# Accumulating products on four column tiles in place of two, with the second pair's sum added by an identity product

## The chip, the cores and the metric

One core of a Trainium2 chip. The metric is the device time of one execution in microseconds (us); lower is better.

The profile calls TensorE PE (PEld is its loading of weights), VectorE DVE and ScalarE ACT. The granted clock is the share of TensorE's full speed that the throttle allows at a moment; in these traces it is 1.00 or 0.50. PSUM is the memory in which products accumulate, in banks. A round is a set of products that run side by side on different column tiles. The path is the chain of work and waits that sets the end.

## The reference, cut to what matters

```python
x = A_x                                     # 8 x 1 x 576, bf16
g = sigmoid((x * gate_w).sum(-1))
a = attention(x @ wq, last 2048 keys and values of each of 16 heads) @ wo    # wo: 4096 x 576
b = gelu(layernorm(B_x) @ w1 + b1) @ w2 + b2                                 # w2: 4608 x 576
return g * a + (1 - g) * b                  # 8 x 576
```

About 134 of the 154 MB that are read are keys and values (16 transfers of 4096 KB and 32 of 2048 KB). The output has only 8 rows: the final sum over `wo` and `w2` is a long series of products with 8 columns of weights (the rows of the batch) against 576 columns of data.

## The kernel before

All products of the two final projections accumulate in one PSUM bank. The 576 output columns are cut into NJ = 2 halves of JN = 288; half j goes to column tile 32j. So two products run at once, on the first two of four column tiles.

```python
class AccGroup:
    def __init__(self, name, mms, deps, cost, after=(), prio=0):
        ...
        def fn(e):
            for i, (lhsT, rhs) in enumerate(grp.mms):
                for j in range(NJ):
                    ins = e.matmul(ps[32 * j:32 * j + 8, BK_ACC, 0:JN], lhsT, rhs[:, JN * j:JN * j + JN],
                                   start=False, stop=True, skip_group_check=True, tile_position=(0, 32 * j))
            return ins
...
def project():                      # output projection: 8 groups of 8 products
    for c in range(4):
        for ch in (c, c + 4):
            dst, d = wo_here[ch // 2]
            mms = [(oT[:, ch, j, :], dst[:, ch % 2, D * j:D * j + D]) for j in range(4)]
            AccGroup("proj%d" % ch, mms, place_done[c] + [d], cost=1.0)
...
def m2_chunk(ci):                   # w2 in 4 chunks; the last in 3 pieces of 4, 4 and 1 rows
    cuts = [0, 4, 8, 9] if ci == FC - 1 else [0, FJ]
    for n, (j0, j1) in enumerate(zip(cuts, cuts[1:])):
        d = dma("sp", w2_fn, ...)
        mms = [(hT[:, FJ * ci + j, :], dst[:, j * D:(j + 1) * D]) for j in range(j0, j1)]
        ops.append(AccGroup("m2_%d_%d" % (ci, n), mms, [o_hT, d], cost=0.16 * (j1 - j0), after=o_m2[-1:]).op)
...
# end: VectorE casts half 0 and ScalarE half 1 out of PSUM, each sends its half
```

A small list scheduler orders the operations of each engine from their estimated costs (`cost`), so a change of cost can move an instruction on PE. Line 757 places the attention output for the projection: sixteen small VectorE copies for each quarter. Line 724 is the sum that comes before it, line 707 the product of probabilities and values. In the changed kernel these lines are 761, 728 and 711, and the accumulate product is at 555 in place of 551.

## Time and profile before

| | before |
|---|---|
| time, first 6 runs | median 366.12 us (365.95 to 368.21) |
| the profiled run | 367.25 us, span 366.0 |
| DMA engines full | 39 of 40 slices |
| PE busy | 243.8 us (67%) |
| copies of line 757 end | 358.93 |
| last piece of w2 lands | 362.55 |
| last product ends | 364.06 |

The lines behind this table stand in the prediction. The table is read from the bottom up: the end is set by what follows the last copies and the last landing, since the transfers before them are full. The profiled run was itself one of the slower runs: it took over 1 us more than the median.

### The profile page before, as it was taken

Reading aid. Unit: us, or ns where it says so; the run is one execution under the profiler, and the core shown is the slowest. Engines: PE = TensorE matmul, PEld = TensorE weight load, DVE = VectorE, ACT = ScalarE, POOL = GpSimd, SP = SyncE. Lnnn points to the kernel's source line nnn. Section 1 sums busy time; section 2 is a strip of 40 time slices with the busy share of each in tenths; the row PEclk is TensorE's granted clock in tenths of the full one; section 3 lists DMA queues with packets and bytes.
Section 4 is the critical chain, followed back from the end, with each engine's and each line's share of the span. In section 5 each row is a group of like instructions: output and inputs, shape, how many; then the busy total and the mean of one; then the engine's idle time right before and its main releaser. Section 6 shows DMA issues by size and latency. Waiting matters only on the chain.

```text
span 366.0 us, 3973 instructions
## 1 busy us (share of the span) xinstructions
PE 243.8 (67%) x1677; PEld 118.2 (32%) x1677; DVE 226.4 (62%) x340; ACT 22.3 (6%) x53; POOL 17.4 (5%) x80
## 2 busy tenths in 40 slices
PE   0269684847598748375969294838968398288777
PEld 0259331312253314122434132314424133144343
DVE  4700995676999090859973453689790839974312
ACT  1010000000010000000100000001000000010000
POOL 4021000001000000010000000000000000000000
PEclk9999998789699969585998778576989598876886
DMA  9999999999999999999999999999999999999994
GB/s 368 449 413 439 417 441 448 412 456 403 455 408 447 414 441 428 426 453 414 458 405 455 405 453 406 458 410 448 415 442 424 439 407 444 420 434 430 423 422 166
DMA packets 9546, 154.58 MB, mean 422 GB/s; under 512 B 1036, under 2 KB 1204, under 8 KB 2744
## 3 DMA queue, kind: packets, MB, share of 16 engines
q1 hardware_dynamic: 9472, 154.29, 98.5%
q8 instruction: 13, 0.21, 0.2%
q10 hardware_dynamic: 56, 0.03, 0.0%
q14 instruction: 5, 0.04, 0.0%
HBM read 154.31 MB, written 0.01 MB: 422 GB/s over the span
## 4 chain that ended last, share of the span: by engine, by line
DMA 65%; DVE 26%; PE 6%; issue 1%; SPq 1%; DVEq 0%
DMA arena<-in_A_k_cache_dram 54%; DVE arena L662 21%; DMA arena<-in_B_w_dram 6%; DMA arena<-in_A_v_cache_dram 6%; PE ps L674 3%; DVE arena L635 2%; PE ps L551 2%; DVE arena L757 1%; PE ps L707 1%; DVE arena L627 1%; DVE arena L593 0%; DVE arena L602 0%; PE ps L724 0%; DVE arena L596 0%; SPq L764 0%
## 5 line engine op out<-in xcount | busy, mean ns | idle before, releaser
L662 DVE STREAM_TRANSPOSE arena<-arena 128x4096 f32<-128x4096 f32 x32 | 140.7, 4424 | 85.6 <-DMA arena<-in_A_k_cache_dram 84.7
L674 PE MATMUL ps<-arena 128*32 128x512 bf16 x512 | 140.3, 437 | 62.9 <-DVE arena L662 62.9
L674 PEld LDWEIGHTS ps<-arena 128*32 128x32 bf16 x512 | 52.0, 105 | 143.7 <-DVE arena L662 68.0
L707 PE MATMUL ps<-arena 128*32 128x512 bf16 x512 | 62.2, 459 | 22.2 <-DVE arena L598 18.7
L707 PEld LDWEIGHTS ps<-arena 128*32 128x32 bf16 x512 | 25.1, 110 | 49.1 <-issue 32.6
L635 DVE STREAM_TRANSPOSE arena<-arena 128x512 bf16<-128x512 bf16 x32 | 30.8, 1021 | 0.0
L724 PE MATMUL ps<-arena 128*128 128x16 f32 x128 | 17.8, 271 | 5.3 <-ACT arena L718 3.5
L724 PEld LDWEIGHTS ps<-arena 128*128 128x128 f32 x128 | 16.3, 200 | 11.6 <-ACT arena L718 9.3
L757 DVE COPY arena<-arena 32x4 bf16<-32x4 bf16 (+1 forms) x80 | 12.9, 161 | 11.4 <-POOL arena L745 9.2
L718 ACT ACTIVATE arena<-ps 128x512 f32<-128x512 f32 x16 | 9.6, 597 | 150.7 <-PE ps L707 150.7
L745 POOL TENSOR_TENSOR arena<-arena 128x8 bf16<-128x8 f32 x30 | 5.8, 229 | 231.2 <-ACT arena L734 231.2
L551 PE MATMUL ps<-arena 128*8 128x288 bf16 (+1 forms) x140 | 12.7, 341 | 2.0 <-DMA arena<-in_B_w_dram 1.7
L508 PE MATMUL ps<-arena 128*128 128x8 bf16 x144 | 10.9, 201 | 2.7 <-DMA arena<-in_B_w_dram 2.7
L593 DVE TENSOR_REDUCE arena<-ps 128x1 f32<-128x512 f32 x8 | 5.5, 691 | 10.8 <-PE ps L674 10.7
L604 ACT ACTIVATE arena<-ps,arena 128x512 bf16<-128x512 f32 x8 | 5.5, 687 | 104.1 <-DVE arena L602 104.1
L508 PEld LDWEIGHTS ps<-arena 128*128 128x128 bf16 x144 | 10.8, 157 | 3.1 <-DMA arena<-in_B_w_dram 3.1
L655 POOL TENSOR_TENSOR arena<-arena 128x32 bf16<-128x32 bf16 x32 | 6.4, 239 | 85.0 <-PE ps L674 75.9
L608 PE MATMUL ps<-arena 128*128 128x32 f32 x16 | 3.7, 318 | 8.6 <-DVE arena L607 8.6
L551 PEld LDWEIGHTS ps<-arena 128*8 128x8 bf16 (+1 forms) x140 | 6.9, 101 | 8.0 <-DMA arena<-in_B_w_dram 2.2
L627 DVE TENSOR_SCALAR arena<-arena 128x512 bf16<-128x512 bf16 x32 | 9.0, 324 | 0.0
L423 PE MATMUL ps<-arena 8*128 8x8 bf16 x8 | 0.6, 171 | 10.8 <-DVE arena L396 6.8
L510 PE MATMUL ps<-arena 128*128 128x8 bf16 x36 | 7.2, 201 | 0.0
(84 smaller groups left out, 77.6 us busy)
## 6 DMA issues: line engine op xcount, KB each, us to landing
arena<-in_A_k_cache_dram SPq DMA_DIRECT2D x16, 4096.0 KB, 25.2
arena<-in_A_v_cache_dram SPq DMA_DIRECT2D x32, 2048.0 KB, 24.1
arena<-in_B_w_dram SPq DMA_DIRECT2D x1, 4608.0 KB, 23.9
arena<-in_A_wo_dram SPq DMA_DIRECT2D x4, 1152.0 KB, 10.1
arena<-in_A_wq_dram SPq DMA_DIRECT2D x1, 4096.0 KB, 13.2
arena<-in_B_w_dram SPq DMA_DIRECT2D x3, 1296.0 KB, 17.4
arena<-in_B_w_dram SPq DMA_DIRECT2D x3, 576.0 KB, 13.0
arena<-in_A_wq_dram SPq DMA_DIRECT2D x1, 512.0 KB, 3.5
```

What stands on the lines that cost most here:

```text
L508: ins = e.matmul(out_, lhsT, yT[:, kt, :], start=(kt == 0), stop=False)
L510: ins = e.matmul(out_, lhsT, yT[:, 4 + c // 2, :], start=False, stop=True)
L551: ins = e.matmul(ps[32 * j:32 * j + 8, BK_ACC, 0:JN], lhsT, rhs[:, JN * j:JN * j + JN], start=False, stop=True, skip_group_check=True, til ...
L627: return e.tensor_scalar(out=dst, in0=view("Pd").rearrange("p (s n) -> p s n", s=2), scalar1=amask[:, a:a + 1], scalar2=None, op0=ALU.mult)
L635: return e.transpose(dst, src)
L655: return e.tensor_tensor(out=dst, in0=src, in1=own, op=ALU.mult)
L662: tr = add("dve", (lambda h=h, kb=kb: lambda e: e.transpose(bass.AP(arena_f, offset=foffs("KT") + kb * SE // 2, ap=[[AST // 2, 128], [4, 1 ...
L674: mm = e.matmul(ps[32 * c:32 * c + 32, 2 * (G % 2) + nb, :], qb[:, G % 2, n, 2 * h + ee, :], rhs, start=(h == 0 and t == 0), stop=(h == 1 ...
L707: mm = e.matmul(ps[c:c + 32, bk, :], PT[:, g % 2, 512 * q + 32 * t:512 * q + 32 * t + 32], slot(s)[:, 512 * t:512 * t + 512], start=(t < 2 ...
L718: u_ev[item] = add("act", lambda e: e.activation(out=EV[:, item % 2, :], in_=ps[:, bk, :].rearrange("p (r d j) -> p r j d", r=4, j=4), fun ...
L724: mm = e.matmul(ps[:, BK_S, OC + 16 * (item % 2):OC + 16 * (item % 2) + 16], EV[:, item % 2, 128 * r:128 * r + 128], i2[:, r, :, :].rearra ...
L757: return [add("dve", (lambda j=j, q=q: lambda e: e.tensor_copy(oT[32 * q:32 * q + 32, ch, j, bs], oN[32 * j:32 * j + 32, q, ch, bs]))(), d ...
```

## The change

The intent: the backlog of products at the end should go at twice the rate, by use of all four column tiles. Products alternate between tiles 0/32 and 64/96. The second pair's sum is copied to SBUF while the last chunk begins, and is added to the first by an fp32 product with a piece of an identity matrix ("the join" below).

```diff
+            def __init__(self, ..., prio=0, split=2):
                     for i, (lhsT, rhs) in enumerate(grp.mms):
                         for j in range(NJ):
-                            ins = e.matmul(ps[32 * j:32 * j + 8, BK_ACC, 0:JN], ..., tile_position=(0, 32 * j))
+                            c = 64 * (i % split) + 32 * j
+                            ins = e.matmul(ps[c:c + 8, BK_ACC, 0:JN], ..., tile_position=(0, c))
 ...
         def project():
             for c in range(4):
-                for ch in (c, c + 4):  (two groups of 8 products)
+                (one group of 16 products over both chunks, cost 1.1)
 ...
-                ops.append(AccGroup("m2_%d_%d" % (ci, n), ..., after=o_m2[-1:]).op)
+                ops.append(AccGroup("m2_%d_%d" % (ci, n), ..., after=o_m2[-1:], split=1 if ci == FC - 1 else 2).op)
+                if ci == FC - 1 and n == 0:
+                    o_ac = add("act", lambda e: e.activation(out=accs[64:128, :], in_=ps[64:128, BK_ACC, 0:JN], func=ACTF.Copy), ...)
+                    def join_fn(e):
+                        for j in range(NJ):
+                            c = 64 + 32 * j
+                            ins = e.matmul(ps[32 * j:32 * j + 8, BK_ACC, 0:JN], i32[c:c + 32, 0:8], accs[c:c + 32, :],
+                                           start=False, stop=True, skip_group_check=True, tile_position=(c, 32 * j))
+                    o_m2.append(add("pe", join_fn, deps=[o_ac], name="join", cost=0.7, after=o_m2[-1:]))
```

(The four tiles are also zeroed at the start instead of two, and the final casts wait for the join.) Because the costs changed, the scheduler also put the last attention sum ahead of the first w2 chunk.

## The prediction

> **What bounds the kernel now.** I read the page first, for what is full over the whole span.
>
> ```profile
> DMA  9999999999999999999999999999999999999994
> q1 hardware_dynamic: 9472, 154.29, 98.5%
> HBM read 154.31 MB, written 0.01 MB: 422 GB/s over the span
> ```
>
> Each digit is a fortieth of the span. The transfers are full in 39 of 40 slices, so the keys, values and weights set the pace until about 359 us. The products that the change touches (line 551) are 12.7 us of PE work, nearly all after 338 us. PE has idle time there, so only what follows the last bytes can move the end. Next, the end of the chain of waits (start us, us, what; the sixteen copies are cut).
>
> ```profile
> 353.24 0.04 issue
> 353.29 1.27 PE ps L551 x18
> 354.56 1.01 PE ps L724 x8
> ...
> 355.59 0.28 DVE arena L745 x2
> ...
> 358.75 0.18 DVE arena L757
> 358.93 0.04 issue
> 358.97 5.09 PE ps L551 x51
> 364.06 0.02 issue
> 364.08 0.45 DVE arena L821
> ```
>
> The last attention sum (line 724) stood on PE behind eighteen w2 products that had waited for their weights until 353.24. Sixteen placing copies followed it, and then a backlog of 52 accumulate products: 16 of the projection, 18 of the third w2 chunk, and 8, 8 and 2 of the last chunk's three pieces. At what rate does PE work it off? I cut the tail into windows (columns: window, length, PE, PEld, DVE, ACT and POOL busy, granted clock, DMA share, GB/s).
>
> ```profile
> 353.29:354.49 1.20, 1.20 (x19) 0.73 (x19) 0.00 (x0) 0.00 (x0) 0.00 (x0) 1.00 1.00 423
> 358.97:362.52 3.55, 3.55 (x30) 1.94 (x32) 0.00 (x0) 0.00 (x0) 0.00 (x0) 0.50 0.46 177
> 362.52:364.06 1.54, 1.52 (x24) 0.88 (x20) 0.00 (x0) 0.00 (x0) 0.00 (x0) 1.00 0.00 0
> ```
>
> At clock 1.00 nine pairs leave PE in about 1.1 us, 0.12 us a pair. At clock 0.50 it is 0.24 us a pair (successive pairs start at 359.409, 359.649 and 359.889 in the trace). So most of the backlog ran at half clock, and the clock recovered only at 362.52.
>
> Then, when does the last data land? The issue of the last piece and its time to landing:
>
> ```profile
> 349.65 0.43 SPq L791 DMA_DIRECT2D arena<-in_B_w_dram  x1
> DMA to landing us min/median/max: 12.9/12.9/12.9
> ```
>
> That is 362.55. In the same way the third chunk lands at 342.22 + 17.2 = 359.42, and the last chunk's first two pieces at 348.80 + 12.0 = 360.80 and 349.18 + 13.0 = 362.18. A last product cannot end before 362.24 + five pair times of 0.12 + 0.29 of its own, about 363.05. Before ended at 364.06. **At most 1.0 us is to be had.**
>
> **What the Trainium skill says.** "TensorEngine Tiling (Array Packing)", Key Properties: different tiles work independently, and a change of tiling mode drains TensorE. The trace agrees on the first: value products in columns 64 to 127 and projection products in columns 0 to 63 ran side by side.
>
> ```profile
> 340.28 1.25 PE L707 MATMUL ps<-arena 128*32 128x512 bf16 x10
> 341.16 0.41 PE L551 MATMUL ps<-arena 128*8 128x288 bf16 x4
> 341.37 0.38 PE L707 MATMUL ps<-arena 128*32 128x512 bf16 x2
> 341.41 0.41 PE L551 MATMUL ps<-arena 128*8 128x288 bf16 x4
> ```
>
> Both kept their pitch (0.215 us a pair of 512, 0.12 of 288), so four tiles should give twice the rate. Of the drain this trace shows nothing.
>
> "TensorE: Matmul & The Clock Gate", Part 1: half clock is the default, and a window of about 3.4 us with enough work lifts it. The trace agrees: the clock changes at 355.69 and 362.52, two windows apart. By my count of streaming time in such windows of the whole trace, a cold one 0.81 full was followed by full clock, one 0.74 full was not; a warm one below 0.38 was followed by half clock.
>
> "FP8 and Floating Point Precision", TensorE Precision Notes: a true fp32 product takes four passes. Here each fp32 product is two records (128 records of line 724 for 64 products); their 16 columns are too few to show the passes.
>
> "PSUM — Partial Sum Buffer", bank collisions: engines may share a bank in different 32-partition quadrants. So ScalarE can copy the second pair (partitions 64 to 127) while PE writes the first. No run yet shows it.
>
> **The change part by part.**
>
> 1. Products alternate between two pairs of columns, except the last chunk's 18 (they stay on two tiles). Eighteen products go from nine rounds to five, sixteen from eight to four. Of the backlog, 8 + 9 rounds become 4 + 5: eight rounds saved, 1.0 us at full clock, 1.9 at half.
>
> 2. The instruction order moves the last attention sum ahead of the first w2 chunk. Its input is ready at 352.08 + 0.60 = 352.68; plus 1.06 of PE, 0.3 and 3.05 of DVE, the copies end near 357.2 instead of 358.93. That takes 1.7 us off the path.
>
> 3. Added: the copy of 64x288 on ScalarE (line 822 does 8x288 in 0.40, same columns, so 0.40), hidden beside the last chunk's first piece; and the join, two fp32 products of 288 columns in four records. Two streaming passes a record is an estimate: 0.24 us a record at full clock, 0.48 at half. A second record of one tile waits for the first, the other tile overlaps only one, so three steps: 0.72 or 1.44 us, perhaps with a drain of 0.2 on either side. It stands on PE ahead of the last two pieces, which makes it path.
>
> After at half clock throughout: second chunk 356.38 + 5 x 0.24 = 357.58; projection + 4 x 0.24 = 358.54; idle until 359.48; third chunk to 360.68; first piece from 360.86 to 361.82; join to 363.26; second piece to 364.22; last pair starting there ends at 364.66. That is 0.6 later than the profiled run of before. At full clock from the first piece on: 360.86 + 0.49 + 0.72 = 362.07, so the landing at 362.18 decides, end 363.05, 1.0 earlier.
>
> **Which clock?** Before kept PE at work from 356.38, with a gap of 0.3, so a sufficiently full window ends by about 362.5 at the latest, often earlier. After works twice as fast, then waits for data, and is steadily busy only from 359.48. A window that is 0.8 full can then end no earlier than about 362.2. The first piece and part of the join mostly run at half clock: ends between 363.7 and 364.7, some 0.2 more with drains. I take 364.2.
>
> And before in its usual run? Its profiled run took 367.25, the median run 366.17. The gap of 1.08 is what lies between 364.06 and the floor of 363.05, so I think the median run is already on the floor, thanks to an earlier lift of the clock, and the 368.21 run is one with a later lift. Then the change cannot win in the median and loses 364.2 - 363.05 = 1.15. I shade this for the chance that the clock is lifted sooner, or that those runs differ by transfers: +0.7, 366.9.
>
> **Rivals.** (a) The gain as intended: the path was compute (5.09 us of PE after the copies), so it shortens to the landing bound, 1.0 us below, about 365.2. For it: the chain. Against it: the time of the median run, and the clock. (b) Nothing visible: the landing of the last piece decides both, 366.2. (c) A slow join: if fp32 products in 32-row tiles drain on every record, or both products run in sequence at half clock, the join is 2 us or more and stands just ahead of the last products, 368.3. (d) Transfers move: earlier or later release of buffers. Against it: issues run 12 us or more ahead of landing, so no change there.
>
> **Range and chances.** From the floor less ordinary spread (365.6) to the slow join (368.3). Two per cent is 7.3 us, more than the whole tail after the last byte and several times any term here; only a surprise in the transfers would reach it. Within 2%: 0.98.
>
> **What would show it.** Right: copies ended near 357.2; line 551 records in groups of four starting together; PE idle before the third chunk until its landing; the clock at 0.50 beyond 362; the join with 0.7 to 1.5 us between first piece and second piece. Wrong: four tiles not overlapping (five rounds taking over 1.5 us at half clock); full clock at 360.8, when rival (a) or (b) holds; ScalarE's copy ending after the first piece, so that PE waits for it; landings moved by more than 0.5 us.

## The result, and the profile after

The changed kernel took **367.15 us** (median of 6 runs, 366.21 to 367.51) against 366.12 of before (6 runs): 1.03 us more. The ratio was 1.0013, with a 95% interval of 0.9988 to 1.0037. Ratios here are the mean time of one kernel's runs over that of the other's of the same rounds, so not quite the ratio of the medians: a single run of before at 368.21 lifts its mean. In five further rounds the changed kernel had 367.48 against 366.60, ratio 1.0023 (1.0010 to 1.0037), which is clear of 1. By the 2% measure it is the same; by the finer one it is slower by about 0.9 us.

Four tiles did what they should. First the chunk's rate. The first line is the first w2 chunk, in the timeline of the changed kernel (start, us, engine, line, operation, count). The next is the same chunk in the timeline of the kernel before:

```profile
355.07 0.78 PE L555 MATMUL ps<-arena 128*8 128x288 bf16 x18
```

```profile
353.29 1.27 PE L551 MATMUL ps<-arena 128*8 128x288 bf16 x18 [0.91 <-DMA arena<-in_B_w_dram]
```

Eighteen products took 0.78 us in place of 1.27, both at full clock: five rounds in place of nine. The chain of waits of the changed kernel ends so:

```profile
358.53 0.04 issue
358.57 3.28 PE ps L555 x21
361.85 1.06 PE ps L813 x4
362.91 0.99 PE ps L555 x10
363.90 0.02 issue
363.92 0.45 DVE arena L841
```

The 5.09 us of products after the copies have become 5.33: 3.28 for the backlog, 1.06 for the join (L813), 0.99 for the last ten products. The last piece landed at 347.81 + 14.5 = 362.31 (issue and time to landing of the changed kernel's last transfer). So the floor here is about 0.2 us below that of the profile before, and the end still lies only 0.16 below. Now the clock, in windows of the changed kernel (window, length, busy time of PE, PEld, DVE, ACT and POOL, granted clock, DMA share, GB/s). Each is 3.41 us long, and they are lined up with the changes of clock:

```profile
346.34:349.75 3.41, 1.25 (x22) 0.39 (x18) 0.99 (x7) 0.00 (x0) 0.00 (x0) 1.00 0.97 411
349.75:353.17 3.42, 3.30 (x16) 1.04 (x16) 0.00 (x0) 0.00 (x0) 0.00 (x0) 0.50 0.99 421
353.17:356.58 3.41, 2.72 (x50) 1.83 (x48) 1.21 (x8) 0.60 (x1) 0.00 (x0) 1.00 1.02 431
356.58:359.99 3.41, 1.83 (x38) 0.80 (x32) 1.62 (x11) 0.00 (x0) 0.00 (x0) 0.50 0.92 376
359.99:363.41 3.42, 3.42 (x32) 1.17 (x26) 0.00 (x0) 0.41 (x1) 0.00 (x0) 0.50 0.22 82
```

PE is busy for 1.25 and 1.83 us of 3.41 in the first and fourth windows, and the windows that follow run at half clock. The third does not fit this reading: PE is busy for 2.72 us there, and half clock follows all the same. Counted as streaming time, the time in which columns of data enter PE (the last section says how), that window is only 0.43 full. In the second of these five the last sixteen value products take 3.51 us in place of 1.90 (the changed kernel first, then the kernel before), so the copies end at 358.53 and not near 357.2:

```profile
349.87 3.51 PE L711 MATMUL ps<-arena 128*32 128x512 bf16 x16 [1.64 <-DMA arena<-in_A_v_cache_dram]
350.14 1.90 PE L707 MATMUL ps<-arena 128*32 128x512 bf16 x16 [0.28 <-DMA arena<-in_A_v_cache_dram]
```

In the last window run the backlog's end, the first piece and the whole join. The kernel before also had half clock from 355.69 to 362.52 in its profile, but with PE busy 2.46 of 3.41 us in the first of those two windows and fully in the second:

```profile
355.69:359.10 3.41, 2.46 (x20) 1.13 (x22) 2.72 (x18) 0.00 (x0) 0.00 (x0) 0.50 0.99 412
359.10:362.52 3.42, 3.42 (x30) 1.85 (x28) 0.00 (x0) 0.00 (x0) 0.00 (x0) 0.50 0.44 167
```

### The profile page after: what moved, and what is told of

Same layout as the page of the kernel before. It is cut to its first block, busy times and chain, and to the rows that moved or that the text cites. A ratio compares the mean times of both kernels' runs of the same rounds, so it can differ in the third digit from the quotient of the medians. Undisturbed runs are those within 1.5% of the kernel's fastest.

```text
span 365.8 us, 3987 instructions
## 1 busy us (share of the span) xinstructions
PE 241.1 (66%) x1683; PEld 114.5 (31%) x1683; DVE 226.3 (62%) x340; ACT 22.7 (6%) x54; POOL 17.4 (5%) x80
## 4 chain that ended last, share of the span: by engine, by line
DMA 60%; DVE 25%; PE 12%; issue 2%; SPq 0%; ACT 0%; DVEq 0%
DMA arena<-in_A_k_cache_dram 54%; DVE arena L666 18%; DMA arena<-in_A_v_cache_dram 6%; PE ps L678 6%; PE ps L711 4%; DVE arena L639 3%; PE ps L555 1%; DVE arena L597 1%; DVE arena L761 1%; DVE arena L631 1%; DVE arena L600 0%; DVE arena L606 0%; PE ps L728 0%; PE ps L813 0%; PE ps L612 0%
## 5 line engine op out<-in xcount | busy, mean ns | idle before, releaser
L728 PE MATMUL ps<-arena 128*128 128x16 f32 x128 | 17.0, 264 | 5.8 <-ACT arena L722 3.9
L728 PEld LDWEIGHTS ps<-arena 128*128 128x128 f32 x128 | 15.5, 191 | 11.7 <-ACT arena L722 9.6
L555 PE MATMUL ps<-arena 128*8 128x288 bf16 (+1 forms) x140 | 10.2, 369 | 2.4 <-DVE arena L761 2.2
L555 PEld LDWEIGHTS ps<-arena 128*8 128x8 bf16 (+1 forms) x140 | 4.4, 100 | 8.3 <-DVE arena L761 3.4
## 6 DMA issues: line engine op xcount, KB each, us to landing
arena<-in_B_w_dram SPq DMA_DIRECT2D x3, 576.0 KB, 14.6
```

The costliest lines, as they stand in the source:

```text
L555: ins = e.matmul(ps[c:c + 8, BK_ACC, 0:JN], lhsT, rhs[:, JN * j:JN * j + JN], start=False, stop=True, skip_group_check=True, tile_position ...
L728: mm = e.matmul(ps[:, BK_S, OC + 16 * (item % 2):OC + 16 * (item % 2) + 16], EV[:, item % 2, 128 * r:128 * r + 128], i2[:, r, :, :].rearra ...
```

## The experiments

Eleven kernels, all timed in 5 rounds beside the kernel before. Runs of one batch share the runs of before: 366.60 median of 9 in the first (runs 1 to 4), 366.58 of 11 in the second (5 to 8), 366.30 of 11 in the third (9 to 11). The three batches ran on chips 10, 9 and 11, so runs of different batches are best compared by their ratios to before. Each kernel left one trace, of one run: what a trace shows of the clock need not hold for the other runs of its kernel.

### 1. The changed kernel again

No edit; it is the reference point for the next three.

> The changed kernel again, so that it shares its rounds with the next three. Theory A (the join stands on PE ahead of the last two pieces, mostly at half clock, and the landing of the last piece is a floor that the kernel before usually reaches): median 0.7 to 1.2 us over that of before, ratio 1.001 to 1.003. Rival C (the difference of the first six runs is chance): medians within 0.4 us of each other.

Measured: 367.48 us (366.72 to 367.62, 5 runs), ratio 1.0023 (1.0010 to 1.0037). Rival C, chance, is out. The last piece landed at 362.62 in its profile. The join (first line), which had begun before that, and the last ten products (second) ran at half clock again, the products until just before their end:

```profile
361.99:363.05 1.06, 1.06 (x7) 0.10 (x6) 0.00 (x0) 0.00 (x0) 0.00 (x0) 0.50 0.03 9
363.05:364.45 1.40, 1.36 (x12) 0.49 (x10) 0.00 (x0) 0.00 (x0) 0.00 (x0) 0.54 0.00 0
```

### 2. Without the join

```diff
-                if ci == FC - 1 and n == 0:
-                    o_ac = add("act", ... accs[64:128] <- ps[64:128] ...)
-                    o_m2.append(add("pe", join_fn, ...))
```

> The changed kernel without the copy on ScalarE and without the join; the second pair's sum is dropped, so the result is wrong on purpose. PE order otherwise as in the changed kernel. Theory A: 1.0 us under the changed kernel, back at the median of before (about 366.1), last products ending within 0.6 us of the landing of the last piece. Rival B (the four tiles themselves cost the time, by letting the clock fall, and the join is hidden): less than 0.4 us under the changed kernel, still 0.7 or more over before. Rival C: no difference from either.

Measured: 366.66 us (366.61 to 366.88), ratio 1.0005 (0.9993 to 1.0018); result wrong. The join costs 0.82 us in the median, so it lies on the path. The median is now that of before in the same rounds (366.60), but not the 366.1 that was expected, where the best runs lie: about 0.55 us remained. The profile of one run suggests where. The last piece landed at 349.24 + 13.2 = 362.44, and the last ten products, ready to run, took 1.36 us:

```profile
354.78:358.20 3.42, 2.12 (x34) 1.13 (x34) 1.77 (x12) 0.00 (x0) 0.00 (x0) 0.50 0.99 415
362.09:363.49 1.40, 1.36 (x10) 0.49 (x10) 0.00 (x0) 0.00 (x0) 0.00 (x0) 0.50 0.00 0
```

The clock was at half throughout these windows, with PE idle for 1.3 us of the first. So A and B may each hold a part; the next runs bear on that. One thing differs from the changed kernel's profile: here the last value products ran at full clock, behind the same shorter projection group.

```profile
349.87 1.90 PE L711 MATMUL ps<-arena 128*32 128x512 bf16 x16 [1.03 <-DMA arena<-in_A_v_cache_dram]
```

### 3. Two tiles in the changed order

```diff
-            def __init__(..., split=2):
+            def __init__(..., split=1):
-                ..., split=1 if ci == FC - 1 else 2).op)
+                ...).op)
-                (the copy and the join)
```

> All products on one pair of column tiles again, no join; only the changed order of PE stays (the last attention sum ahead of the first w2 chunk). Theory A: copies end over 1 us earlier than before in a profile of equal clock, but the end is the landing or the backlog at half clock, as before: ratio 0.998 to 1.001. If the order were what cost time: 0.7 us or more over before. Rival B: as before, ratio 1.000, and under the run without join by 0.7 us.

Measured: 366.11 us (366.02 to 366.62), ratio 0.9993 (0.9979 to 1.0007). The order costs nothing and may win a little. With nine rounds in place of five, PE was busy for 3.35 of 3.41 us in a window at half clock, and the clock came back in time:

```profile
356.08:359.49 3.41, 3.35 (x30) 1.84 (x32) 0.76 (x5) 0.00 (x0) 0.00 (x0) 0.50 0.96 398
359.49:362.02 2.53, 2.12 (x35) 1.31 (x31) 0.00 (x0) 0.00 (x0) 0.00 (x0) 1.00 0.45 169
362.02:362.84 0.82, 0.78 (x10) 0.36 (x10) 0.00 (x0) 0.00 (x0) 0.00 (x0) 1.00 0.00 0
```

The last ten products took 0.78 us against 1.36 without the join on four tiles. That is 0.58 us, and the medians differ by 0.55. In these two profiles the slower arrangement finishes earlier because it is clocked twice as high when it matters. The pair does not settle it alone: the number of tiles differs as well as the clock, and the windows do not cover the same work (this one begins at 356.08, that of run 2 at 354.78).

### 4. The add on VectorE in place of the join

```diff
-    o_ac = add("act", ... out=accs[64:128, :], in_=ps[64:128, BK_ACC, 0:JN] ...)
-    (join)
+    o_ac = add("act", ... out=accs[0:64, :], in_=ps[64:128, BK_ACC, 0:JN] ...)
-    (two final casts)
+    o_fin = add("dve", lambda e: e.tensor_tensor(out=out_sb[0:64, :], in0=ps[0:64, BK_ACC, 0:JN], in1=accs[0:64, :], op=ALU.add), ...)
```

> Four tiles kept, the identity products taken away: ScalarE copies the second pair's sum from partitions 64 to 127 to partitions 0 to 63 of SBUF, and the final VectorE operation adds it while it casts. Result correct. Theory A: like the run without join, median 366.0 to 366.2 (the final add may take 0.1 us more than the cast), and a narrow spread, since nine of the 26 rounds of backlog are gone; ratio 0.997 to 0.999. Rival B: over before by 0.7 us. Rival C: as before.

Measured: 366.56 us (366.33 to 367.10), ratio 1.0004 (0.9991 to 1.0017), correct. The expectation of 366.0 to 366.2 failed. (Its nine rounds saved are eight by the prediction's own count.) It is like the run without the join, as A says, and like it lies about half a microsecond above two tiles. The add itself took 0.45 us in place of the cast's 0.45, so it is not the reason. In its profile the clock was at half until 362.80.

### 5. The changed kernel with the idle time filled

```diff
+    def fill(n): n products of 32 weights by 320 columns into PSUM bank 0 (never read)
+    5 after the third projection group, 11 after the first w2 chunk, 4 after the last projection group
```

> The changed kernel with 20 filler products (320 columns, into an unused PSUM bank, never read) in three places where PE waits for data, so that its windows are full and the clock stays up; result correct. Theory A+clock (half of the loss is the join, half is that faster products leave PE idle and so at half clock): granted clock 1.00 in the join and the last five rounds; median 0.6 to 1.2 us under the changed kernel, about 0 to 0.3 over the floor of 366.05. Rival (the clock does not matter, only the join's length in instructions): unchanged against the changed kernel, ratio to before 1.002. Rival (fillers only add work): later than the changed kernel.

Measured: 366.33 us (366.07 to 366.57), ratio 0.9993 (0.9980 to 1.0006); the changed kernel's ratio was 1.0023 in the batch before. Twenty useless products took the loss away, with join and all. In its profile (the filler between the chunks; then the join, then the last ten products):

```profile
353.96:356.22 2.26, 1.86 (x26) 1.12 (x15) 1.91 (x12) 0.00 (x0) 0.00 (x0) 1.00 0.99 421
361.28:362.09 0.81, 0.66 (x7) 0.10 (x6) 0.00 (x0) 0.00 (x0) 0.00 (x0) 1.00 0.29 108
362.09:362.91 0.82, 0.78 (x10) 0.36 (x10) 0.00 (x1) 0.00 (x1) 0.00 (x0) 1.00 0.00 0
```

The copies ended at 356.99, near the predicted 357.2. The join took 0.66 us and was over before the second piece was there: it landed at 347.43 + 14.6 = 362.03. In this profile the join is hidden at full clock; at half clock (run 1) it lies on the path. The rival that only the number of instructions counts is out: its ratio of 1.002 lies outside the interval.

### 6. The add on VectorE, filled as well

```diff
+    fill(5), fill(11), fill(4) as above, and fill(2) between the first and second piece of the last chunk
```

> Four tiles, the add on VectorE in place of the join, and 22 fillers. Theory: last ten products at clock 1.00, median 365.9 to 366.1, 0.5 us under the same kernel without fillers (ratio 1.0004 there), spread under 0.4; ratio to before 0.998 to 0.999. Rival (something else in four tiles costs the half microsecond): ratio stays at 1.0004.

Measured: 366.69 us (366.28 to 367.99, 6 runs), ratio 1.0004 (0.9989 to 1.0020). A miss, and the rival's ratio of 1.0004 (something else in four tiles costs the half microsecond) is the one that came. The profiled run was one at full clock to the end, at 366.28 near the floor, but four of the six runs took 366.64 or more. Two of these four had a mean clock of 0.850 and 0.851 over the span, no lower than the fast ones. Against the rival speaks run 5, which has four tiles too and lost nothing; the intervals of 5 and 6 overlap, so this stays open.

### 7. Two tiles, filled

```diff
+    fill(8) after the first w2 chunk, fill(2) after the first piece of the last (on the kernel of 3)
```

> Two tiles in the changed order with 10 fillers. Theory: two tiles already keep PE full enough, so the median stays at the floor, 366.0 to 366.1, with fewer runs above 366.3 than without fillers; ratio 0.998 to 0.9995. If fillers cost time by themselves: over the run without fillers (0.9993) by 0.3 us or more.

Measured: 366.44 us (366.09 to 367.00), ratio 0.9996 (0.9983 to 1.0008). The expected 366.0 to 366.1 failed: no gain over two tiles without fillers. Four of the five runs lie above 366.3, against one of five in 3. Against 3 (0.9993) the difference is within the intervals, so it is inconclusive whether fillers cost anything there.

### 8. The join twice

```diff
+    o_m2.append(add("pe", join_fn, deps=[o_ac], name="join2", cost=0.7, after=o_m2[-1:]))
```

> The changed kernel with the join done twice (the second pair's sum is added twice, so the result is wrong on purpose). Theory A: the second join adds two more steps of two overlapping records, 0.44 us each at half clock, 0.24 at full clock, all on the path: 0.5 to 0.9 us over the changed kernel, ratio to before 1.0037 to 1.005. Rival (the join is hidden behind the landing of the last pieces): ratio stays at 1.0023.

Measured: 368.11 us (367.32 to 368.61, 6 runs), ratio 1.0038 (1.0024 to 1.0052), wrong. That is 0.0015 of 366.6, or 0.55 us, over the ratio of the changed kernel; by medians 0.63. The rival that the join is hidden is out. In its profile both joins together took 2.02 us at half clock against 1.06 for one, so each costs about 1 us there. Why the medians differ by less is not shown:

```profile
361.94:363.96 2.02, 2.02 (x11) 0.38 (x9) 0.00 (x0) 0.00 (x0) 0.00 (x0) 0.50 0.04 13
```

### 9. The floor: few products after the copies

```diff
+    if ci >= FC - 2: mms = mms[:1]      (8 products in place of 36 in the last two chunks; on the kernel of 3)
```

> Two tiles in the changed order, but of the last two w2 chunks only one product for each piece (eight products in place of 36); the transfers stay. Wrong on purpose. Theory (the landing of the last piece is a floor under every version of the tail): 365.8 to 366.1, no more than 0.3 us under the two-tile run with all its products (366.11), ratio to before 0.997 to 0.999. Rival (the tail's products are still the bound at the floor): 1 us or more lower, 365 or less.

Measured: 366.16 us (366.09 to 367.10, 6 runs), ratio 0.9990 (0.9971 to 1.0009), wrong. Taking away 28 products of the tail gains nothing against two tiles with all of them (366.11; by ratio 0.9990 against 0.9993). The profile shows PE waiting for each landing:

```profile
360.88 0.29 PE L555 MATMUL ps<-arena 128*8 128x288 bf16 x2 [1.09 <-DMA arena<-in_B_w_dram]
362.39 0.65 PE L555 MATMUL ps<-arena 128*8 128x288 bf16 x4 [1.22 <-DMA arena<-in_B_w_dram]
```

So about 366.1 is the floor that the transfers set: fewer products after the copies do not go below it. One run of six still took 367.10, so part of the spread comes from something other than these products.

### 10. The kernel before, filled

```diff
+    fill(5) ahead of the first w2 chunk, fill(5) ahead of the second
```

> The kernel before with 10 fillers at two places where PE waits (ahead of the first and of the second w2 chunk). Theory (the slower runs of before, 366.6 to 368.2, are runs in which the clock was lifted late): median 366.0 to 366.3, no run above 366.7, ratio 0.9975 to 0.9995. Rival (those runs are transfers that landed later): the spread of before stays, 366.0 to 367.4.

Measured: 366.20 us (366.09 to 366.62, 6 runs), ratio 0.9990 (0.9970 to 1.0009), correct. The eleven runs of before beside it had 366.12 to 368.26, four of them over 366.7; none of the six did. Its profile worked off the backlog at full clock:

```profile
358.87:362.17 3.30, 2.74 (x44) 1.82 (x44) 0.00 (x0) 0.00 (x0) 0.00 (x0) 1.00 0.57 228
362.17:362.99 0.82, 0.78 (x10) 0.36 (x10) 0.00 (x1) 0.00 (x1) 0.00 (x0) 1.00 0.00 0
```

Over the 31 runs of before in the three batches, the 12 above 366.7 had a mean clock of 0.838 over the span, the 14 at 366.30 or below 0.849. Both support that the slower runs of before are runs of late clock, though no trace shows where in the run the clock was low, save the profiled one. Six runs are too few to exclude luck: with 4 of 11 slow, six good ones in a row come about one time in fifteen ((7/11) to the sixth power is 0.066).

### 11. The add on VectorE, filled, less the last two fillers

```diff
-    fill(2) between the first and second piece of the last chunk
```

> The VectorE-add kernel with fillers again, without the two that stood between the first and the second piece of the last chunk. If those two held up the last products in some runs: median 366.1, no run above 366.7, ratio 0.998 to 0.9995. If the slow runs of the earlier try came from the transfers or from the other fillers: ratio 1.000 again.

Measured: 366.57 us (366.18 to 367.59, 6 runs), ratio 1.0001 (0.9980 to 1.0021). The two fillers were not the reason. Three runs lie at 366.18 to 366.30 with a mean clock of 0.850 over the span; the other three, at 366.84 to 367.59, had 0.835 or 0.836. So the slow ones go with a lower clock somewhere in the run here, unlike two of those in 6. No trace of such a run exists, and where it was low stays open.

No version is shown to beat before: two tiles in the changed order (0.9993), the filled changed kernel (0.9993) and the filled kernel before (0.9990) all have intervals that hold 1. They share the floor, and before is on it in about half of its runs (18 of its 37 at 366.30 or below; of the changed kernel's 11 timed runs, one).

## Why the prediction was right or wrong

The result, 367.15, lies in the range and 0.25 above the point; the sign, against the intent of the change, was right.

- **At most 1.0 us to be had, and the median run already has it.** Right for the first six runs and the third batch, half right for the others. The floor kernel (9) came to 366.16 with most of the tail's products gone. The medians of before were 366.12 in the first six runs, 366.60, 366.58 and 366.30 in the batches (366.32 over all 37), so in two batches the median run had half a microsecond to gain. On the runs at the floor halving the backlog could gain nothing: it ends in waiting for the last landings. (The prediction's sum for the end of the last product adds up to 363.13, not 363.05. The fifth pair starts after four pair times, which gives 363.01; measured were 0.78 us for the ten products in run 10.)
- **Four tiles, twice the rate.** Right: 0.78 us in place of 1.27 for eighteen products.
- **The order takes 1.7 us off the path.** Right at full clock (copies end at 356.99 in run 5), not in the profile after (358.53). I had taken the last value product from the profile before, 1.90 us at full clock. The shorter projection group left PE idle in the window ahead of it (1.25 us of 3.41 busy), and it ran at half clock for 3.51. I had applied the argument of the clock to the tail alone. That the shorter group did it is argued from this trace only: behind the same group it took 3.17 and 3.25 in runs 1 and 8, but 1.90 in 2 and 4, where the clock changed at other times. With the copies late, PE also had no idle time before the third chunk, which the prediction had named as a sign; in run 1 it had 0.35 us.
- **The join, 1.44 us in three steps, with drains of 0.2 on either side.** The mechanism was right: on PE, ahead of the last two pieces, path at half clock and not at full. The size was over by a third, by the prediction's 1.44 without drains. The records of the two products came in pairs, 7 ns apart, so two steps and not three: records start at 361.783 and 362.225 in the profile after, and the next product at 362.844. That is 1.06. Steps within the joins of run 8 are 0.48 apart, so the second step's 0.62 holds about 0.14 more than streaming; ahead of the join were 0.13 of wait. Both gaps stand at a change of tiling mode, so they are probably the drain. The prediction said that the trace of before shows nothing of it, but there the first product of line 724 starts 0.216 us after the last of line 551 (354.271 to 354.487), against 0.12 between pairs before. Without the join the median fell by 0.82 us.
- **The clock: faster products, more idle time, half clock for longer.** Right for the changed kernel: run 5 shows that filling the idle time removes the whole loss. How much of it the clock costs without a join is less sure. Run 3 against run 2 gives 0.55 us, but fillers did not bring the versions with the add on VectorE down (1.0004 and 1.0001 with them, 1.0004 without). The form was not always the one forecast, a late lift: in run 1's profile the clock was full from 354.09 to 360.92, which the prediction had named as a sign of (a) or (b), and then fell for the join. Nor do the traces hold to the window that must be 0.8 full (last section).
- **The sum.** +1.15 over the median run was worked out and shaded to +0.7; measured were +1.03 in the first six runs and +0.88 in the five of run 1. Both lie between the two figures. In its parts the estimate erred both ways, the join too dear by 0.4 us and the copies too early by 1.3, so that the sum came out this close is partly luck.
- **Rivals.** (a) failed by the floor and the clock, (b) by the join, (c) by the join's real length, (d) by landings of the last piece within 0.4 us of each other in all traces (362.29 to 362.66), one of each kernel; the slow runs that left no trace are not covered.

What stays open: why the versions with the add on VectorE keep some slow runs though filled (6, 11), and so how much of the 0.55 us between runs 2 and 3 is the clock.

## What to carry to other kernels

Before speeding up a tail, work out the floor that the last landing sets and see whether the usual run, not the profiled one, is already on it. A faster engine that then waits may be given a lower clock, and what must still run after the wait, such as a final join, pays for it. A step that was added for the sake of speed belongs where the engine waits anyway, or on an engine that is off the path.

## What the Trainium skill lacked or had wrong

- "TensorE: Matmul & The Clock Gate", Part 1, says that a busy window lifts the gate, and gives no measure for how full. Counted as streaming time (288 columns of bf16 take 0.12 us at full clock and 0.24 at half, fp32 records twice that; side by side counts once), windows of the trace of before at half clock (cold) and filled to 0.81 and 0.82 were followed by full clock, those at 0.66 and 0.74 were not. Other traces set the limit lower or blur it: 0.69 (run 2, from 330.89) and 0.76 (run 1, from 350.68) were followed by full clock, 0.76 in run 9 (from 152.02) was not. A window at full clock (warm) and filled to 0.40 stayed warm, those at 0.37 and 0.35 fell to half; in the changed kernel one at 0.43 fell as well, so the lower limit is not sharp in this count.
- The same page does not say how small products count. In run 8 a window filled to 0.91 by this count was not followed by full clock; more than half of it were join records of 32 rows and 8 columns. That such records count for less is only a guess from this one window.
- The same page's advice to keep PE dense lacks the reverse case: fewer rounds in a group went with half clock for what came next in the profile of run 2 (run 3, with all its rounds, was 0.55 us faster), and 20 products whose result nobody reads took the loss of the changed kernel away (run 5), though much the same fillers gained nothing in runs 6 and 11.
- "TensorEngine Tiling (Array Packing)", Key Properties, names the drain at a change of tiling mode without a size. The gaps at such changes here were about 0.13 us going into the join and 0.14 coming out, at half clock, and 0.10 going in at full clock (run 5; in the trace of before, 0.10 at 354.27).
- "FP8 and Floating Point Precision", TensorE Precision Notes, agrees: the records of the join start 0.246 us apart at full clock, which is twice the 0.12 us of 288 columns of bf16: two passes in each of two records, four for a product.
- "PSUM — Partial Sum Buffer", bank collisions, agrees: in the changed kernel ScalarE read partitions 64 to 127 from 360.94 to 361.34 while PE wrote 0 to 63 of the same bank, and the result was correct.
